# Attention and two feed-forward parts on one core: the second part's weights split early and kept in DRAM, the rests on VectorE, elu as a maximum

## The chip, the cores and the metric

One Trainium2 chip, of which the kernel uses one core with its five engines: TensorE (PE, with its weight loads as PEld), VectorE (DVE), ScalarE (ACT), GpSimd (POOL) and SyncE (SP), whose queue issues all of this kernel's DMAs. The metric is the device time of one execution in microseconds (us); several runs give a median.

## The reference

Attention with rotary positions runs over 4 batches of 8 heads with 576 tokens of 64 values. Its result, 2304 tokens of 512 values, goes through two feed-forward parts. The weights are float64, everything else is float32.

```python
x = attention(q, k, v)                              # 2304 x 512
h = x @ w_in                                        # 512 -> 2048
g = np.where(h > 0.0, h, np.exp(np.minimum(h, 0.0)) - 1.0)   # elu
x = (g @ w_out).astype(np.float32)                  # 2048 -> 512
a, b = x @ w1, x @ w2                               # 512 -> 1024 each
out = ((a * b @ w3) @ w_out2).astype(np.float32)    # 1024 -> 1024 -> 512
```

## The kernel before

Every float32 operand of TensorE stands as two tiles, the upper 12 bits (hi) and the exact rest (lo), and three matmuls (hi·hi, hi·lo, lo·hi) make one product. The matrix `w3 @ w_out2` (called W) is made once, so that the second part is `((x @ w1) * (x @ w2)) @ W`.

Weights come as 64-bit words, in parts of 128 partitions by 512 words (512 KB). `weight_steps` turns a part into its hi and lo in six steps: `rebase` on ScalarE (L104), `shift`, `low` and `sign` on VectorE (L107, L110, L113), `high` on ScalarE (L117) and `rest`, a subtraction, on GpSimd (L121). Three working tiles `wr` are shared by all parts; the result goes into the buffer that held the raw words.

The program has three stages.

- Attention: 16 units (pairs of heads) of 9 slots each, in an order written out by hand. GpSimd turns q and k here. Along with it the first parts of `w_in` and `w_out` are fetched and split, one every 9 slots from slot 10 on (`paced`); the constant `PF` says for how many of the 16 columns f of the first part both weights are made here, 5 before.
- First feed-forward part: five tiles of tokens (512, 512, 512, 384, 384), each with 16 slots f. `part_h` makes 128 columns of h (12 matmuls, L532) and the elu: a minimum on VectorE (L543), exp and minus one on ScalarE (L544, L545), a maximum and sum on VectorE (L547), then the split of g, hi on ScalarE (L77) and lo (L73) on GpSimd in the first tile of tokens and on VectorE in the others. `part_y` adds the product with `w_out` (12 matmuls, L559) for the slot before. In the first tile of tokens the remaining parts of `w_in` and `w_out` are loaded and split (`load_in_out`).
- In the last tile of tokens all 40 parts of the second feed-forward part's weights are loaded into the buffers that `w_in` and `w_out` leave, and split there: 8 of `w_out2` (`load_o`), 16 of `w3` (`load_3`), 8 each of `w1` and `w2` (`load_ab`). `part_w` makes a block of rows of W (24 matmuls, L590) in each of the last 8 slots. The second feed-forward part follows, with 24 matmuls for a and b (L532) and 12 or 9 for y (L647) a slot.

In the two feed-forward stages the order on each engine is not the program's: a scheduler places the instructions when the kernel is built, by its own table of costs. On the chip each engine then takes its instructions in just that order, so an instruction that waits holds up all that stands behind it on its engine; the same holds for DMAs on SP's queue.

Of the kernel before, what the change touches and what calls it, by code (L numbers as in the profile page):

```python
# [7 lines left out]
F32 = mybir.dt.float32  # L8
# [10 lines left out]
P = 128  # L19
NKC = 5  # parts of the keys, 128 and at the end 64  # L20
SK = S + 64  # the keys with the last 64 of them in front once more
SCALE = 1.0 / 8.0
SIGN = -(2**31)
PAIRS = ((0, 0), (0, 1), (1, 0))  # the products of (hi, lo) with (hi, lo) that float32 keeps

# Slots of a unit (a pair of heads) in the attention, counted from its first: 4 parts of the queries for each head, and
# the last 64 queries of both. Work on the unit itself:
NORM = (2, 7)  # reciprocals of the sums, of the first 256 queries and of the others
SPREAD = (3, 9)  # their broadcast over d
NTURN = (5, 11)  # its transpose  # L30
PV = (
    (5, 0, (0,)), (6, 0, (1,)), (7, 0, (2, 3)), (8, 0, (4,)),
    (10, 1, (0,)), (11, 1, (1,)), (12, 1, (2, 3)), (13, 1, (4,)),
)  # slot, part of the queries, parts of the keys
LOAD_V = 6  # and on those that follow it: loads, and the steps of the rope of k and q
LOAD_QK = 4
ROPE = ((-1, 0, 1, 1, 4), (-5, -4, -3, -3, 2))
STACK = 4
# The first unit, of which nothing runs ahead
FIRST = ((0, 1, 4), (0, 0, 0, 1, 2), (0, 0, 3, 3, 4), 2)  # L40
KD = 420  # keys from here on are turned by the second engine
WARM = 27
FILL = (4, 2, 2)
EVAC_ACT = (1, 0, 0, 1, 0, 0, 0, 0, 1, 0, 1, 0)  # which copies from PSUM are ScalarE's, in turn

# Weights: how many parts of w_in and w_out are split during the attention, from which slot on, and the steps' slots
PF, PF_AT, PF_STEP, STEPS, DLEAD = 5, 10, 9, (0, 1, 2, 2, 3, 8), 6
NA = 2 * PF
# In the last tile of tokens of the first feed-forward part: when the weights of the second are loaded, per part of f
LOAD_O = (0, 1, 1, 2, 3, 3, 4, 5)  # L50
LOAD_3, PART_W, LOAD_AB, AB_STEP = 5, 8, 10, 2
DEEP = 3  # parts of w3 held at once


@with_exitstack
def kernel(
# [9 lines left out]
    w_pools = [wa_p]  # L66
    wr_p = ctx.enter_context(tc.tile_pool(name="wr", bufs=3))

    def split(dst, src, hi_eng, lo_eng):
        """dst[:, 0] = src to 12 bits, dst[:, 1] = the exact rest."""  # L70
        hi, lo = dst[:, 0], dst[:, 1]
        copy_hi(hi, src, hi_eng)
        lo_eng.tensor_tensor(lo, src, hi.bitcast(F32), op=ALU.subtract)  # L73
# [16 lines left out]

    def weight_steps(at_, raw, put):
        """Float64 words to two tiles' worth of float32: 12 bits of 24, and the rest.

        The high word read as float32 has a float64 exponent's upper 8 bits: times 2**-112 it is
        rebased by -896 (what is too small for float32 goes to 0), and 3 bits to the left it is
        float32's layout, without the sign."""
        words = raw.bitcast(I32).rearrange("p (n t) -> p n t", t=2)
        lo, hi = words[:, :, 0], words[:, :, 1]
        r = wr_p.tile([P, 512], F32, tag="wr", name="wr")
        i = r.bitcast(I32)  # L100
        made = []

        def rebase():
            act.activation(r, hi.bitcast(F32), ACTF.Abs, scale=2.0**-112)  # L104

        def shift():
            dve.tensor_scalar(i, i, 3, None, op0=ALU.logical_shift_left)  # L107

        def low():
            dve.scalar_tensor_tensor(i, lo, 29, i, op0=ALU.logical_shift_right, op1=ALU.bitwise_or)  # L110

        def sign():
            dve.scalar_tensor_tensor(i, hi, SIGN, i, op0=ALU.bitwise_and, op1=ALU.bitwise_or)  # L113

        def high():
            made.append(slot(at_, F32R, [P, 2, 512], "w"))
            act.activation(made[0][:, 0], r, ACTF.Copy)  # L117
            put(made[0])

        def rest():  # L120
            pool.tensor_tensor(made[0][:, 1], r, made[0][:, 0].bitcast(F32), op=ALU.subtract)  # L121

        return rebase, shift, low, sign, high, rest

    def load_w(i, src, to, key):
        for f in weight_steps(i, fetch_w(i, src), lambda t: to.__setitem__(key, t)):
            f()
# [6 lines left out]

    # ------------------------------------------------ attention, and w3 @ w_out
    with ExitStack() as c1:
# [35 lines left out]
        def rope(u, w):  # L172
            """Steps of the turn of q or k by their positions, and of its split."""
            if u not in hls:
# [20 lines left out]
        def first_load(u):  # L195
            """In the order of their use: the first half of the scores, the other, and the other queries."""
            for w in (0, 1):
# [7 lines left out]
        def part(u, w, at_, to, eng, hi_eng, lo_eng):  # L205
            """Steps for some columns; the scale goes with the split."""
            s, c, t = (SCALE, 1.0)[w], COLS[w].start, TAB[w].start
# [34 lines left out]
        def diagonal(u):  # L242
            """The last 64 queries of each head, against its own keys only."""
            for j in range(2):
                h = slice(64 * j, 64 * j + 64)
                copy_hi(diag[units.index(u) % 2][h, :, h], hls[u][h, :, 512:S].bitcast(F32), pool)

        def stack(u):
            """Of each head [128 = (q_hi, q_lo)], [k_hi, k_lo] and [k_lo, k_hi], on the partitions."""
            st = stacks[u] = st_p.tile([P, 2, 3, S], F32R, tag="st", name="st")  # L250
# [9 lines left out]

        # ---- attention: of a pair of heads 128 queries each, and then the 64 last of both at once
        HALF = ((0, 256), (256, 320))
        sums_t, S_t, pr_t, pt_t = {}, {}, {}, {}

        def scores(g):
            u, c, j = g
            s = S_t[g] = ps_s.tile([P, 2, 512], F32, tag="s", name="s")
            if c == 4 or u == units[0]:
                # the halves one by one: of both heads with the diagonal, or of one
                d, h = diag[units.index(u) % 2], slice(64 * j, 64 * j + 64) if c < 4 else slice(0, P)  # L270
# [133 lines left out]
        def paced(n, i_, to, key, src):  # L404
            """The weights of src, fetched ahead of slot n, and the split's steps in the slots from there."""
            steps, raw = [], []
# [4 lines left out]
            def step(i):  # L411
                if i == 0:
                    steps.extend(weight_steps(i_, raw[0], lambda t: to.__setitem__(key, t)))
                steps[i]()
# [52 lines left out]
        def warm_up(n):  # L467
            """Keeps TensorE's clock up while it would wait."""
            ps = ps_t.tile([P, 512], F32, tag="pt", name="warm") if n else None
            for _ in range(n):  # L470
                pe.matmul(ps[:, :P], warm, warm, start=True, stop=True)
# [34 lines left out]

    # ------------------------------------------------ the two feed-forward parts
    with ExitStack() as c2:
        pool2 = lambda name, bufs: c2.enter_context(tc.tile_pool(name=name, bufs=bufs, reuse_waits="tile"))
        xt_p = pool2("xt", 4)  # L510
        w_pools.append(pool2("w", 1))
        g_p = pool2("g", 2)
        e_p = pool2("e", 2)
# [13 lines left out]
        def project(ps, w, x, n):  # L527
            """ps = (w as [c, 128 of f]).T @ x"""
            i = 0
# [8 lines left out]
        def part_h(ti, f, x):  # L538
# [3 lines left out]
            e = e_p.tile([P, n], F32, tag="e", name="e", padded_shape=[P, 512])  # L542
            dve.tensor_scalar(e, ps[:, :n], 0.0, None, op0=ALU.min)  # L543
            act.activation(e, e, ACTF.Exp)  # L544
            act.activation(e, e, ACTF.Copy, bias=-1.0)  # L545
            g = e
            dve.scalar_tensor_tensor(g, ps[:, :n], 0.0, e, op0=ALU.max, op1=ALU.add)  # L547
            t = g_p.tile([P, 2, n], F32R, tag="g", name="g", padded_shape=[P, 2, 512])
            split(t, g, act, dve if ti else pool)
            gs[ti, f] = t  # L550
# [19 lines left out]
        wo, w3_t = {}, {}  # L570

        def load_ab(f):
            i = 16 + 2 * DEEP + 2 * f
            i = i if i < 32 else i - 24
            load_w(i, w1[f], wa, f)
            load_w(i + 1, w2[f], wb, f)

        def load_o(j):
            load_w(j, w_o2[j], wo, j)

        def load_3(i):
            for z in range(2):
                load_w(8 + 2 * (i % DEEP) + z, w3[i][:, 512 * z:512 * z + 512], w3_t, (i, z))

        def part_w(i):
            """Rows of w3 @ w_o2."""
            ps = ps_h.tile([P, 512], F32, tag="h", name="w")
# [20 lines left out]
        for n, (ti, f) in enumerate(seq):  # L608
# [5 lines left out]
            if n >= 1:  # L614
                part_y(*seq[n - 1])
            for task, i in tasks.pop(n - len(seq) + NF, ()):
                task(i)
# [112 lines left out]
```

## Time and profile before

| | |
|---|---|
| time, median of 3 runs (lowest, highest) | 1089.44 us (1088.63, 1090.51) |
| span of the profiled execution | 1087.1 us |
| time beside the span (median less span) | 2.3 us |
| PE / PEld busy | 96% / 80% |
| DVE / ACT / POOL busy | 57% / 43% / 34% |
| HBM read / written | 64.68 MB / 4.72 MB |

The profile gives the profiled execution's span, from its first to its last instruction; no other time of that execution is on the page, so the time that lies around it is taken as the difference to the median. The page's busy share of PE counts a matmul from its start to its modelled end, including time in which it overlaps the next, so the pitch at which matmuls follow one another says more than the share. Attention ends at about 317 us, the first feed-forward part at about 788 us.

### The profile page before, as it was taken

To read this page: it belongs to the slowest core of one execution; us is meant where nothing else is said; L and a number is where in the kernel's file an instruction comes from. 1 tells how busy PE (TensorE), PEld (TensorE's weight loads), DVE (VectorE), ACT (ScalarE), POOL (GpSimd) and SP (SyncE) were. 2 spreads that over 40 slices of the span, in tenths; PEclk is the share of its full clock that TensorE was granted. 3 is DMA by queue.
4 is the path that set the end of the run, shared out by engine and by line. 5 is a ranking of instruction groups with operands and counts; after the bars stand their busy time and mean duration, and the time that the engine had idled before them with its cause. 6 is when DMAs were issued, how large, how long until landed. Compare 5 with 4: busy or idle time off the path is not lost. (4 is left out here: it accounts for less than half of the span.)

```text
span 1087.1 us, 14661 instructions
## 1 busy us (share of the span) xinstructions
PE 1048.0 (96%) x5590; PEld 865.3 (80%) x5590; DVE 621.9 (57%) x982; ACT 467.3 (43%) x921; POOL 365.4 (34%) x336
## 2 busy tenths in 40 slices
PE   9999999999998789999999999889899999999998
PEld 7777677677766568888888999778788888889997
DVE  5778788777659975335335346997971313122211
ACT  3566667666636554334334335654451111112121
POOL 5788898877226551001000001343450000000000
PEclk7899999999999999999999999999999999999999
DMA  5777787867481000000000005446500100001000
GB/s 164 207 223 222 216 226 224 220 195 198 120 339 48 0 1 1 1 1 1 1 1 1 1 1 159 122 127 190 159 20 1 39 1 25 15 1 39 1 30 30
DMA packets 34870, 96.90 MB, mean 89 GB/s; under 512 B 4208, under 2 KB 5872, under 8 KB 34800
## 3 DMA queue, kind: packets, MB, share of 16 engines
q1 hardware_dynamic: 34800, 95.96, 29.6%
q8 instruction: 44, 0.72, 0.3%
q14 instruction: 26, 0.21, 0.1%
HBM read 64.68 MB, written 4.72 MB: 64 GB/s over the span
## 5 line engine op out<-in xcount | busy, mean ns | idle before, releaser
L559 PE MATMUL y<-g,w 128*128 128x512 f32 (+1 forms) x960 | 218.0, 374 | 23.8 <-ACT g L77 16.8
L559 PEld LDWEIGHTS y<-g,w 128*128 128x128 f32 x960 | 176.3, 191 | 54.8 <-ACT g L77 22.0
L532 PE MATMUL h<-xt,w 128*128 128x512 f32 (+1 forms) x960 | 212.2, 368 | 1.1 <-DVE e L547 1.1
L532 PEld LDWEIGHTS h<-xt,w 128*128 128x128 f32 x960 | 175.1, 188 | 24.8 <-DVE e L547 1.5
L73 POOL TENSOR_TENSOR xt<-xT,xt 128x512 fp32r<-128x512 f32 (+1 forms) x20 | 25.5, 1273 | 446.1 <-DVE xt L79 446.1
L298 ACT ACTIVATE pr<-s,nm 128x576 f32<-128x576 f32 x144 | 107.0, 743 | 101.8 <-DVE nm L294 100.9
L121 POOL TENSOR_TENSOR w<-wr,w 128x512 fp32r<-128x512 f32 x72 | 102.5, 1424 | 124.6 <-ACT w L117 119.8
L294 DVE TENSOR_REDUCE nm<-s 128x1 f32<-128x576 f32 x144 | 108.6, 754 | 24.8 <-PE s L282 12.0
L634 DVE TENSOR_TENSOR a<-b,a 128x512 f32<-128x512 f32 (+1 forms) x40 | 25.5, 637 | 157.5 <-PE b L532 156.8
L532 PE MATMUL a<-xt,w 128*128 128x512 f32 (+1 forms) x480 | 107.8, 368 | 2.7 <-DVE xt L73 2.7
L532 PE MATMUL b<-xt,w 128*128 128x512 f32 (+1 forms) x480 | 106.8, 367 | 0.0
L647 PE MATMUL y<-W,g 128*128 128x512 f32 x432 | 105.2, 391 | 0.2 <-DVE g L73 0.2
L544 ACT ACTIVATE e<-e 128x512 f32<-128x512 f32 (+1 forms) x80 | 47.0, 588 | 135.7 <-DVE e L543 135.6
L532 PEld LDWEIGHTS a<-xt,w 128*128 128x128 f32 x480 | 88.1, 188 | 15.5 <-DVE xt L73 3.1
L330 PEld LDWEIGHTS ptp<-idt,pr 128*128 128x128 f32 x576 | 63.4, 144 | 46.2 <-issue 24.7
L282 PE MATMUL s<-st 128*128 128x288 f32 x480 | 95.1, 316 | 4.0 <-DMA st<-hl 3.8
L532 PEld LDWEIGHTS b<-xt,w 128*128 128x128 f32 x480 | 87.6, 188 | 11.3
L330 PE MATMUL ptp<-idt,pr 128*128 128x128 f32 x576 | 96.4, 291 | 0.0
L647 PEld LDWEIGHTS y<-W,g 128*128 128x128 f32 x432 | 80.8, 188 | 16.7 <-DVE g L73 0.6
L543 DVE TENSOR_SCALAR e<-h 128x512 f32<-128x512 f32 (+1 forms) x80 | 50.6, 633 | 63.1 <-PE h L532 62.9
L547 DVE SCALAR_TENSOR_TENSOR e<-h,e 128x512 f32<-128x512 f32 (+1 forms) x80 | 50.7, 634 | 57.7 <-ACT e L545 57.7
L180 POOL TENSOR_TENSOR raw_qk<-raw_qk,tab 128x640 f32<-128x640 f32 (+1 forms) x56 | 82.5, 1482 | 2.3
(302 smaller groups left out, 1371.1 us busy)
## 6 DMA issues: line engine op xcount, KB each, us to landing
st<-hl SPq DMA_DIRECT2D x60, 288.0 KB, 4.5
raw<-w_ SPq DMA_DIRECT2D x32, 512.0 KB, 4.1
raw_qk<-k_ SPq DMA_DIRECT2D x15, 640.0 KB, 5.7
raw_qk<-q_ SPq DMA_DIRECT2D x15, 576.0 KB, 5.2
st<-hl SPq DMA_DIRECT2D x60, 144.0 KB, 4.2
raw<-w_in_ SPq DMA_DIRECT2D x16, 512.0 KB, 5.1
raw<-w_out_ SPq DMA_DIRECT2D x16, 512.0 KB, 5.8
out_<-ev SPq DMA_DIRECT2D x18, 256.0 KB, 2.1
```

Source lines behind the costliest of these rows:

```text
L121: pool.tensor_tensor(made[0][:, 1], r, made[0][:, 0].bitcast(F32), op=ALU.subtract)
L180: pool.tensor_tensor(r[:, z], r[:, z], tab[:, w, z, TAB[w]], op=ALU.mult)
L282: pe.matmul(s[:, n, :288], st[:, j, 0, c * P:c * P + P], st[:, j, z, n * 288:(n + 1) * 288], start=(z == 1), stop=(z == 2),)
L294: dve.tensor_reduce(nm, s[:, :, :288], axis=AX.XY, op=ALU.max, negate=True)
L298: act.activation(pr_t[u, c][:, j].rearrange("p (n i) -> p n i", n=2), s[:, :, :288], ACTF.Exp, bias=nm, accum_out=sums_t[u, hf][:, at_:at_ ...
L330: pe.transpose(pt[:, kc], pr[:, at_:at_ + P], idt)
L532: pe.matmul(ps[:, :n], w[:, a, cc * P:(cc + 1) * P], x[cc][:, c], start=(i == 0), stop=(i == 11))
L543: dve.tensor_scalar(e, ps[:, :n], 0.0, None, op0=ALU.min)
L544: act.activation(e, e, ACTF.Exp)
L547: dve.scalar_tensor_tensor(g, ps[:, :n], 0.0, e, op0=ALU.max, op1=ALU.add)
L559: pe.matmul(ys[ti][o][:, :n], wout[f][:, a, o * P:(o + 1) * P], g[:, c], start=(f == 0 and i == 0), stop=(f == NF - 1 and i == 2),)
L647: pe.matmul(outs[ti][o], g[:, a, o * P:(o + 1) * P], wW[f][:, c], start=(f == 0 and i == 0), stop=(f == NG - 1 and i == 2),)
```

## The change

- The sign, shift and other steps of a weight part stay; the `rest` of weights that are split in the feed-forward stages goes to VectorE (in attention it stays on GpSimd). The lo half of g is VectorE's in the first tile of tokens too.
- The elu becomes `max(exp(min(h, 0)) - 1, h)`: a ReLU of -h and an exp on ScalarE, and one pass on VectorE.
- `PF` goes from 5 to 6: 12 parts of `w_in` and `w_out` are split in attention, 20 are left for the first tile of tokens.
- The 40 parts of the second feed-forward part's weights are fetched and split one a slot from slot 17 of the 80 on (`early`), through a ring of three buffers (`stage`) that raw words and results share, and the result is written to DRAM. In the last tile of tokens `load_o`, `load_3` and `load_ab` only load it back (`again`).

```diff
-PF, PF_AT, PF_STEP, STEPS, DLEAD = 5, 10, 9, (0, 1, 2, 2, 3, 8), 6
+PF, PF_AT, PF_STEP, STEPS, DLEAD = 6, 10, 9, (0, 1, 2, 2, 3, 8), 6
+EARLY, EARLY_STEP, STAGES = 17, 1, 3
...
         def high():
-            made.append(slot(at_, F32R, [P, 2, 512], "w"))
+            made.append(stage_p.tile([P, 2, 512], F32R, tag="stage", name="w") if at_ is None else
+                        slot(at_, F32R, [P, 2, 512], "w"))
...
         def rest():
-            pool.tensor_tensor(made[0][:, 1], r, made[0][:, 0].bitcast(F32), op=ALU.subtract)
+            rest_eng.tensor_tensor(made[0][:, 1], r, made[0][:, 0].bitcast(F32), op=ALU.subtract)
...
-            dve.tensor_scalar(e, ps[:, :n], 0.0, None, op0=ALU.min)
-            act.activation(e, e, ACTF.Exp)
-            act.activation(e, e, ACTF.Copy, bias=-1.0)
+            act.activation(e, ps[:, :n], ACTF.Relu, scale=-1.0)
+            act.activation(e, e, ACTF.Exp, scale=-1.0)
             g = e
-            dve.scalar_tensor_tensor(g, ps[:, :n], 0.0, e, op0=ALU.max, op1=ALU.add)
+            dve.scalar_tensor_tensor(g, e, -1.0, ps[:, :n], op0=ALU.add, op1=ALU.max)
...
-            split(t, g, act, dve if ti else pool)
+            split(t, g, act, dve)
...
+        def early(key, src):
+            raw = stage_p.tile([P, 512], I64, tag="stage", name="raw")
+            nc.sync.dma_start(raw, src)
+            done = {}
+            for f in weight_steps(None, raw, lambda t: done.__setitem__(0, t), dve):
+                f()
+            kept[key] = kept_p.tile([P, 2, 512], F32, tag="kept_%s_%d_%d" % key, name="kept")
+            nc.sync.dma_start(kept[key], done[0].bitcast(F32))
+        def again(i, key, to, at_):
+            to[at_] = slot(i, F32R, [P, 2, 512], "w")
+            nc.sync.dma_start(to[at_].bitcast(F32), kept[key])
...
         def load_o(j):
-            load_w(j, w_o2[j], wo, j)
+            again(j, ("o", j, 0), wo, j)
...
             if n >= 1:
                 part_y(*seq[n - 1])
+            if n >= EARLY and (n - EARLY) % EARLY_STEP == 0 and ahead:
+                early(*ahead.pop(0))
```

The new kernel's lines have other numbers: in it L110 is the shift of a weight part, L113 low, L116 sign and L125 the rest; L552 is the elu's pass on VectorE, L76 the lo half of g, L582 the fetch and L587 the store of an early part.

On VectorE in the first tile of tokens, a piece of the kernel before (shift, low and sign of weight parts, and the elu's two passes L543 and L547):

```order
L107 TENSOR_SCALAR wr<-wr 128x512
L110 SCALAR_TENSOR_TENSOR wr<-raw,wr 128x512
L113 SCALAR_TENSOR_TENSOR wr<-raw,wr 128x512
L107 TENSOR_SCALAR wr<-wr 128x512
L543 TENSOR_SCALAR e<-h 128x512
L547 SCALAR_TENSOR_TENSOR e<-h,e 128x512
L110 SCALAR_TENSOR_TENSOR wr<-raw,wr 128x512
```

The same place now (`w` is a weight part, `g` the elu's result):

```order
L110 TENSOR_SCALAR wr<-wr 128x512
L125 TENSOR_TENSOR w<-wr,w 128x512
L116 SCALAR_TENSOR_TENSOR wr<-raw,wr 128x512
L76 TENSOR_TENSOR g<-e,g 128x512
L113 SCALAR_TENSOR_TENSOR wr<-raw,wr 128x512
L110 TENSOR_SCALAR wr<-wr 128x512
L552 SCALAR_TENSOR_TENSOR e<-e,h 128x512
L125 TENSOR_TENSOR w<-wr,w 128x512
```

The rests (L125) and the lo half of g (L76) stand between the other passes, and each elu has one pass (L552) where it had two.

On VectorE from the second tile of tokens on, where before nothing of weights stood, the pattern is now (one early part a slot; every few slots a second elu stands between two parts):

```order
L110 TENSOR_SCALAR wr<-wr 128x512
L113 SCALAR_TENSOR_TENSOR wr<-raw,wr 128x512
L116 SCALAR_TENSOR_TENSOR wr<-raw,wr 128x512
L552 SCALAR_TENSOR_TENSOR e<-e,h 128x512
L125 TENSOR_TENSOR w<-wr,w 128x512
L76 TENSOR_TENSOR g<-e,g 128x512
```

The elu and the lo half of g of a slot stand behind passes that wait for an early part's words; the first early rest is placed behind the 14th elu of 80 and the 40th behind the 60th, 40 parts beside 46 elus.

On SP's queue the early parts stand as a fetch and a store in turn:

```order
L582 DMA raw<-w_o_ 128x512 x2
L587 DMA kept<-w 128x1024
L582 DMA raw<-w_o_ 128x512
L587 DMA kept<-w 128x1024
L582 DMA raw<-w_o_ 128x512
```

Two fetches go ahead; from then on a fetch waits for the store of the part two before it, whose buffer it takes, and the next store stands behind it.

## Rows read from the trace of the kernel before

**Rows 1.** The page's head and its busy times.

```profile
span 1087.1 us, 14661 instructions
PE 1048.0 (96%) x5590; PEld 865.3 (80%) x5590; DVE 621.9 (57%) x982; ACT 467.3 (43%) x921; POOL 365.4 (34%) x336
```

**Rows 2.** Busy time of each engine by stretches (first the stretch and its length, then busy us and number of instructions, and at the end the granted clock, the DMA share and GB/s): the end of attention to the end of weight work in the first tile of tokens; from there to the last tile; the last tile and the start of the second part; the rest.

```profile
317.37:403.15 85.78, 69.47 (x291) 52.79 (x288) 79.25 (x95) 50.42 (x85) 51.16 (x35) 1.00 0.14 53
403.15:671.20 268.05, 268.05 (x1293) 235.73 (x1292) 119.88 (x187) 103.60 (x180) 15.82 (x12) 1.00 0.03 10
671.20:816.40 145.20, 133.57 (x631) 116.01 (x630) 126.47 (x176) 74.87 (x135) 59.05 (x41) 0.98 0.43 129
816.40:1087.10 270.70, 266.18 (x1260) 231.01 (x1259) 66.74 (x105) 46.37 (x82) 9.24 (x8) 1.00 0.05 18
```

**Rows 3.** Pieces of the chain of work that ended last (start us, us, what): twelve matmuls over 512 columns and twelve over 384.

```profile
816.39 2.72 PE a L532 x12
...
999.07 2.10 PE a L532 x12
```

**Rows 4.** The first stretch again, of PE's matmuls alone: those of line 532 (h), then those of line 559 (y).

```profile
317.37:403.15 85.78, 36.39 (x143) 1.00 0.14 53
...
317.37:403.15 85.78, 37.91 (x144) 1.00 0.14 53
```

**Rows 5.** Groups of PE's matmuls in the third stretch, by shape (number, busy us, mean ns, idle time before them).

```profile
L590 PE MATMUL w<-w 128*128 128x512 f32 x192 | 45.8, 391 | 0.2 <-ACT w L117 0.2
L559 PE MATMUL y<-g,w 128*128 128x384 f32 x169 | 37.1, 363 | 8.5 <-DVE g L73 6.3 <-ACT g L77 2.2
L532 PE MATMUL h<-xt,w 128*128 128x384 f32 x137 | 26.2, 336 | 0.0
L532 PE MATMUL a<-xt,w 128*128 128x512 f32 x49 | 12.6, 392 | 2.7 <-DVE xt L73 2.7
L532 PE MATMUL b<-xt,w 128*128 128x512 f32 x48 | 11.5, 389 | 0.0
L647 PE MATMUL y<-W,g 128*128 128x512 f32 x36 | 9.0, 393 | 0.2 <-DVE g L73 0.2
```

**Rows 6.** Groups of VectorE in the first stretch, by shape; the last row is from the second stretch, the lo half of g where GpSimd is silent.

```profile
L110 DVE SCALAR_TENSOR_TENSOR wr<-raw,wr 128x512 int32<-128x512 int32 x22 | 23.6, 1075 | 0.2
L107 DVE TENSOR_SCALAR wr<-wr 128x512 int32<-128x512 int32 x22 | 21.5, 982 | 0.0
L113 DVE SCALAR_TENSOR_TENSOR wr<-raw,wr 128x512 int32<-128x512 int32 x22 | 20.8, 947 | 0.2
L547 DVE SCALAR_TENSOR_TENSOR e<-h,e 128x512 f32<-128x512 f32 x14 | 9.5, 683 | 4.0 <-ACT e L545 4.0
L543 DVE TENSOR_SCALAR e<-h 128x512 f32<-128x512 f32 x14 | 9.4, 681 | 1.9 <-PE h L532 1.9
...
L73 DVE TENSOR_TENSOR g<-e,g 128x512 fp32r<-128x512 f32 x32 | 22.1, 692 | 20.9 <-ACT g L77 20.2
```

**Rows 7.** The timeline of ScalarE, VectorE and GpSimd (start us, us, what): one weight part that meets no other, its rebase, shift, low, sign, high and rest.

```profile
661.59 0.67 ACT L104 ACTIVATE wr<-raw 128x512 f32<-128x512 f32 x1
662.49 0.42 DVE L107 TENSOR_SCALAR wr<-wr 128x512 int32<-128x512 int32 x1
662.94 0.69 DVE L110 SCALAR_TENSOR_TENSOR wr<-raw,wr 128x512 int32<-128x512 int32 x1
663.66 0.69 DVE L113 SCALAR_TENSOR_TENSOR wr<-raw,wr 128x512 int32<-128x512 int32 x1
664.39 0.64 ACT L117 ACTIVATE w<-wr 128x512 fp32r<-128x512 f32 x1 [0.70 <-DVE wr L113]
665.11 1.30 POOL L121 TENSOR_TENSOR w<-wr,w 128x512 fp32r<-128x512 f32 x1 [11.19 <-ACT w L117]
```

**Rows 8.** The timeline of GpSimd and of VectorE in the first tile of tokens: two passes of GpSimd and the VectorE passes that run beside them.

```profile
336.75 1.49 POOL L121 TENSOR_TENSOR w<-wr,w 128x512 fp32r<-128x512 f32 x1
341.92 1.33 POOL L73 TENSOR_TENSOR g<-e,g 128x512 fp32r<-128x512 f32 x1 [0.38 <-ACT g L77]
...
337.11 1.68 DVE L110 SCALAR_TENSOR_TENSOR wr<-raw,wr 128x512 int32<-128x512 int32 x1
342.01 1.52 DVE L107 TENSOR_SCALAR wr<-wr 128x512 int32<-128x512 int32 x1
```

**Rows 9.** Who waited for whom over the whole span (us in total, times, longest): PE's waits in the two feed-forward stages.

```profile
PE y L559 <- ACT g L77: 16.8, 10, 3.1
PE a L532 <- DVE xt L73: 2.7, 1, 2.7
```

**Rows 10.** From issue to landing: the 512 KB weight loads of the last tile of tokens, then the 256 KB writes of the result.

```profile
DMA to landing us min/median/max: 3.4/4.1/5.5
...
DMA to landing us min/median/max: 2.0/2.1/3.3
```

**Rows 11.** Busy times by stretches of 25 us in attention, as in rows 2: two with weight parts beside it and two without.

```profile
175.00:200.00 25.00, 24.39 (x174) 17.30 (x173) 19.10 (x35) 16.24 (x38) 22.05 (x21) 1.00 0.87 230
200.00:225.00 25.00, 24.33 (x177) 18.12 (x176) 19.20 (x37) 17.65 (x43) 21.00 (x23) 1.00 0.64 186
225.00:250.00 25.00, 24.62 (x181) 17.76 (x179) 17.44 (x32) 14.98 (x36) 20.52 (x21) 1.00 0.80 217
250.00:275.00 25.00, 25.00 (x186) 18.73 (x183) 17.89 (x35) 17.06 (x39) 19.38 (x21) 1.00 0.62 168
```

More of the change, by code (lines that the diff above doesn't have):

```diff
@@ L67 @@
     wr_p = ctx.enter_context(tc.tile_pool(name="wr", bufs=3))
+    kept_p = ctx.enter_context(tc.tile_pool(name="kept", bufs=1, space=bass.MemoryType.DRAM))
     def split(dst, src, hi_eng, lo_eng):
@@ L89, in fetch_w, with weight_steps @@
         return raw
-    def weight_steps(at_, raw, put):
+    def weight_steps(at_, raw, put, rest_eng):
         words = raw.bitcast(I32).rearrange("p (n t) -> p n t", t=2)
@@ L120, in rest @@
         def rest():
-            pool.tensor_tensor(made[0][:, 1], r, made[0][:, 0].bitcast(F32), op=ALU.subtract)
+            rest_eng.tensor_tensor(made[0][:, 1], r, made[0][:, 0].bitcast(F32), op=ALU.subtract)
         return rebase, shift, low, sign, high, rest
     def load_w(i, src, to, key):
-        for f in weight_steps(i, fetch_w(i, src), lambda t: to.__setitem__(key, t)):
+        for f in weight_steps(i, fetch_w(i, src), lambda t: to.__setitem__(key, t), dve):
             f()
@@ L412, in step @@
                 if i == 0:
-                    steps.extend(weight_steps(i_, raw[0], lambda t: to.__setitem__(key, t)))
+                    steps.extend(weight_steps(i_, raw[0], lambda t: to.__setitem__(key, t), pool))
                 steps[i]()
@@ L511 @@
         w_pools.append(pool2("w", 1))
+        stage_p = pool2("stage", STAGES)
         g_p = pool2("g", 2)
@@ L570 @@
         wo, w3_t = {}, {}
+        kept = {}
+        def early(key, src):
[9 more added lines that the diff above has]
+            nc.sync.dma_start(to[at_].bitcast(F32), kept[key])
         def load_ab(f):
@@ L574, in load_ab @@
             i = i if i < 32 else i - 24
-            load_w(i, w1[f], wa, f)
-            load_w(i + 1, w2[f], wb, f)
+            again(i, ("a", f, 0), wa, f)
+            again(i + 1, ("b", f, 0), wb, f)
         def load_o(j):
-            load_w(j, w_o2[j], wo, j)
+            again(j, ("o", j, 0), wo, j)
         def load_3(i):
             for z in range(2):
-                load_w(8 + 2 * (i % DEEP) + z, w3[i][:, 512 * z:512 * z + 512], w3_t, (i, z))
+                again(8 + 2 * (i % DEEP) + z, ("3", i, z), w3_t, (i, z))
+        ahead = [(("o", j, 0), w_o2[j]) for j in range(8)]
+        ahead += [(("3", i, z), w3[i][:, 512 * z:512 * z + 512]) for i in range(8) for z in range(2)]
+        ahead += [t for f in range(NG) for t in ((("a", f, 0), w1[f]), (("b", f, 0), w2[f]))]
         def part_w(i):
@@ L720 @@
     }
-    nc = bacc.Bacc("TRN2", target_bir_lowering=False, num_devices=1)
+    nc = bacc.Bacc("TRN2", target_bir_lowering=False, num_devices=1, dynamic_dma_scratch_size=2048)
     args = [
```

## The prediction

> **What bounds the kernel now.** I read the page's busy times first, then stretches of the span, then the groups and the timeline in the stretches where something is lost. PE is busy 96% of 1087.1 us [rows 1], so the first question is how much of that is pitch and how much is waiting. The chain that ended last shows the pitch where nothing disturbs it: twelve matmuls over 512 columns take 2.72 us, 0.2267 us each, and twelve over 384 columns 2.10 us or a little less, on average 0.1735 us each over a slot [rows 3]. A slot of the first part (24 matmuls) is therefore 5.44 us at 512 tokens and 4.16 us at 384.
>
> Held against the stretches [rows 2], two lose time. From 317.37 to 403.15 us PE did 143 + 144 matmuls over 512 columns [rows 4]; at 0.2267 us these need 65.1 us, and they took 85.78, so 20.7 us are lost. From 671.20 to 816.40 it did 306 matmuls over 384 columns and 325 over 512 [rows 5]: 306 x 0.1735 + 325 x 0.2267 = 126.8 us in 145.2, so 18.4 us are lost. In the second and the fourth stretch PE has no gap worth the name: it is busy 268.05 of 268.05 and 266.18 of 270.70 us, the latter with its tail. So 39.1 us can be had, in two places, and nothing elsewhere after attention.
>
> Both are the stretches in which weight parts are split, and in both VectorE is the full engine: 79.25 of 85.78 us and 126.47 of 145.20 [rows 2]. The reader is to see two things in its groups. Shift, low and sign take 982, 1075 and 947 ns on average in the first stretch [rows 6], but 0.42, 0.69 and 0.69 us for a part that meets nobody [rows 7]. And the long ones stand beside a pass of GpSimd: a low of 1.68 us beside GpSimd's pass of 1.49 us, a shift of 1.52 us beside one of 1.33 us [rows 8]. The elu's passes, which read PSUM, keep their 681 and 683 ns in the same stretch [rows 6]. So what is lost is not that VectorE has too much to do but that GpSimd's passes hold its weight passes up, and the elu behind them in the same queue is late. PE waits for g: 16.8 us in ten waits, the longest 3.1 [rows 9].
>
> **The first tile of tokens.** GpSimd's rests and its lo half of g go to VectorE. Each costs 0.69 us there (0.692, the lo half of g in quiet, rows 6). VectorE's bill for the tile was 22 parts and the elus, 84.8 us by the five groups of rows 6. Now it is 20 parts x (0.42 + 3 x 0.69) = 49.8 us and 16 slots x 2 x 0.69 = 22.1 us, together 71.9 us for 16 slots of PE, 87.0 us. VectorE is no longer full. The elu's chain loses one VectorE pass (0.68) and keeps three ScalarE passes. As a cover for what stays late at the start and in the queue I keep one wait of the longest kind, 3.1 us [rows 9]. The stretch gives 20.7 - 3.1 = 17.6 us; from 20.7 (nothing late) down to -10 (the second rival).
>
> **The last tile of tokens.** 40 x 2.49 us of VectorE and 40 passes of GpSimd leave it; only loads of the same 512 KB stay. They take 4.1 us [rows 10] and have time: the last buffer that W's first block needs is free four slots of 4.16 us before it is used, and the w3 buffers come round after three blocks of W. The switch to the second part needs x split on VectorE; that wait was 2.7 us [rows 9], and I keep it. 18.4 - 2.7 = 15.7 us; bounds 18.4, and 10 if the first two blocks of W each wait for a load of 4.1 us.
>
> **Attention.** Two more parts take 18 slots; 144 slots take 317 us, so 18 are 40 us. PE did 174 and 177 instructions in 25 us with weights beside it, 181 and 186 without [rows 11]: 4.4% of 40 us, +1.7 us, from 0 to 3.
>
> **The early parts.** This is the new cost. By work alone there is room: a part adds 2.49 us to VectorE, which with 2 x 0.69 of elu makes 3.87 of 5.44 us, and 1.3 to ScalarE; DMA was at 3% [rows 2]. What can bind is the ring of three buffers. A fetch waits for the store of the part two before, so two parts pass in the time of one round: fetch, six steps, store. The fetch is 4.1 us (3.4 to 5.5, rows 10). The steps from the start of rebase to the end of high are 3.44 us, and 0.08 + 0.69 for the rest, 4.2 us [rows 7]; elu passes that stand between them add none to two of 0.60, I take 0.9. The store has no row. A 256 KB write lands in 2.1 us; 512 KB cannot be faster than the 2.0 that was the fastest, and at twice the length it is 4.2 [rows 10]; I take the middle, 3.1. Four handovers of about 0.1 make 0.4. Sum 12.7 us a round, between 9.9 and 15.5.
>
> The order on VectorE ties 40 parts to 46 elus, so a round has 2 x 46/40 = 2.3 slots, 12.5 us (at 384 columns eight parts beside twelve elus, three slots, 12.5 again). A shorter round costs nothing, since the ring then waits for PE. A longer one holds the elu behind a pass that waits for words, and PE with it: each us above 12.5 costs 20 us over 20 rounds. At 12.7 it is 4 us; the bounds are 0 and 60.
>
> The Trainium skill (DMA: Bandwidth & Descriptors, section Measured under Bandwidth) gives 6.15 us for 1 MB from HBM and 0.95 for 64 KB, issued another way; an estimate between them for 512 KB is 3.4 us. As the price of the store it would make the round 13.0 us and the loss 10 us; the trace has no such store.
>
> **The sum.** Against the profiled span: 1087.1 - 17.6 - 15.7 + 1.7 + 4 = 1059.5 us. Around it lie 2.3 us, the median of 1089.44 less the span. Forecast 1062 us (1061.8).
>
> **The rivals.**
>
> The ring binds in part: a round of 13.0 to 14.2 us. For it speaks that my sum already lies at the limit and that fetch and store share SP's queue, each store standing behind a fetch that waits. Against it, the fetch need not meet another one: with one store and one fetch in 6.2 us it should land nearer to 3.4. Loss 10 to 34 us instead of 4, so 1068 to 1092, more likely in the lower half.
>
> Slower than before: the ring binds in full, at a fetch of 5.5 us, a store of 4.2, two elu passes in between: 15.5 us. Then 20 x 3.0 = 60 us are lost and the span is 1115.5, the time 1118. The point from which it decides is where the loss eats 17.6 + 15.7 - 1.7 = 31.6 us, a round of 14.1 us. The rows of the loads speak against it: 5.5 is the longest of all, taken while two or more loads ran together. The Trainium skill (DMA: Bandwidth & Descriptors, Latency and other measured facts) puts HBM's access latency at 0.2 us on average and 2 us under high load; by that rule, with fetch and store both 1.8 us longer, a round would be 16.3 us and this rival true. No run here shows a loaded store; DMA at 3% before and some 170 GB/s now is less than the 230 GB/s that attention moves [rows 11].
>
> VectorE stays slow: its weight passes are long for another reason than GpSimd (the 64-bit stride of the raw words). Then the first tile costs 20 x (0.98 + 1.08 + 0.95 + 0.69) + 22.1 = 96 us, 10 more than now, and the time is 1087.1 + 10.3 - 15.7 + 1.7 + 4 + 2.3 = 1090, no change. Against it stands the part of rows 7, with the same stride and short passes.
>
> **How the numbers follow.** Forecast 0.70; ring in part 0.20; ring in full 0.06; VectorE slow 0.04. The best case, nothing lost anywhere and no price in attention, is 1087.1 - 39.1 + 2.3 = 1050.3; I begin the range at 1051. Upwards it takes in most of the ring in part, to 1079. Two runs of one kernel differ by up to 0.2% here, so that is what a measurement can tell from no change: 1087.3 to 1091.6. Faster: the forecast, nearly all of the ring in part and some of the slow VectorE, 0.92; same 0.03; slower 0.05.
>
> **What would show it.** In the profile after: shift, low and sign at 0.42, 0.69 and 0.69 us after attention, and no GpSimd there but for x; PE at 110 matmuls per 25 us from 325 us on; in the last tile no weight passes on VectorE and blocks of W without gaps; stores that land in about 3 us. The forecast is wrong if ScalarE's rebase waits for fetches (a wait of rebase for `raw` of more than a few us in total) and PE's count falls between the second and the fourth tile of tokens, which is the ring, or if PE still waits for g in the first tile.

## The result: 1089.04 to 1052.45 us, and the profile after

The new kernel takes 1052.45 us, the median of four runs (1051.51 to 1053.71); the kernel before took 1089.04 us on the same chip (1086.97 to 1090.51). The ratio is 0.9666, 95% interval [0.9646, 0.9686]. The forecast was 1062 us with a range from 1051 to 1079.

The head of the new kernel's page and its busy times, beside [rows 1], and its bytes:

```profile
span 1050.8 us, 14641 instructions
...
PE 1037.8 (99%) x5590; PEld 865.4 (82%) x5590; DVE 568.3 (54%) x978; ACT 463.7 (44%) x921; POOL 257.9 (25%) x260
...
HBM read 85.66 MB, written 25.69 MB: 106 GB/s over the span
```

PE's 5590 matmuls are the same and fill 99% of a span that is 36.3 us shorter. GpSimd is busy 107.5 us less. The 40 stores and the 40 loads back add 21 MB in each direction. The profiled run took 1052.59 us, so 1.8 us lie around the span.

Busy times by stretches (the columns of [rows 2]): the first tile of tokens, the second to the middle of the fourth, the rest of the fourth, the last tile with the start of the second part, and the rest.

```profile
320.00:400.00 80.00, 80.00 (x354) 66.04 (x353) 74.03 (x131) 54.05 (x95) 3.27 (x2) 1.00 0.21 77
400.00:580.00 180.00, 180.00 (x805) 150.26 (x804) 123.50 (x202) 102.80 (x176) 5.88 (x4) 1.00 0.52 181
580.00:672.00 92.00, 92.00 (x533) 92.00 (x532) 44.25 (x78) 42.28 (x83) 2.29 (x2) 1.00 0.43 149
672.00:817.00 145.00, 145.00 (x685) 125.62 (x684) 34.45 (x52) 28.93 (x52) 5.47 (x4) 1.00 0.30 98
817.00:1050.80 233.80, 229.29 (x1098) 200.52 (x1096) 56.80 (x90) 41.44 (x74) 6.82 (x6) 1.00 0.06 21
```

In the first line PE issues 354 matmuls in 80 us; at the undisturbed pitch of [rows 3], 0.2267 us, 80 us hold 353. So nothing is lost, although VectorE still works 74 of 80 us. In the last tile, the fourth line, VectorE falls to 34 of 145 us.

VectorE's groups in the first tile of tokens, 317 to 395 us (the view of [rows 6]):

```profile
L113 DVE SCALAR_TENSOR_TENSOR wr<-raw,wr 128x512 int32<-128x512 int32 x22 | 16.2, 735 | 0.0
L116 DVE SCALAR_TENSOR_TENSOR wr<-raw,wr 128x512 int32<-128x512 int32 x22 | 15.1, 686 | 0.0
L125 DVE TENSOR_TENSOR w<-wr,w 128x512 fp32r<-128x512 f32 x22 | 15.1, 686 | 0.7 <-ACT w L121 0.7
L552 DVE SCALAR_TENSOR_TENSOR e<-e,h 128x512 f32<-128x512 f32 x15 | 10.2, 683 | 2.8 <-ACT e L550 2.6
L110 DVE TENSOR_SCALAR wr<-wr 128x512 int32<-128x512 int32 x22 | 9.3, 422 | 0.4 <-ACT wr L107 0.4
```

Shift 422 ns for 982, low 735 for 1075, sign 686 for 947: the durations of the lone part of [rows 7], now with 22 parts in a row. Low's mean is above 0.69 us because one of its passes, beside GpSimd's split of x at 391 us, took 1.78 us. The elu's pass has not changed (683).

The weights' transfers on the page (KB each, and at the end the median us from issue to landing): stores, loads back, and fetches of early parts (32 of the 40).

```profile
kept<-w SPq DMA_DIRECT2D x40, 512.0 KB, 2.6
w<-kept SPq DMA_DIRECT2D x40, 512.0 KB, 3.3
...
raw<-w_ SPq DMA_DIRECT2D x32, 512.0 KB, 3.6
```

Waits over the whole span (total, times, longest): all of PE's own, then those of ScalarE's rebase (L107) for a fetch.

```profile
PE s L286 <- DMA st<-hl: 4.3, 10, 0.9
PE s L278 <- ACT hl L80: 3.0, 1, 3.0
PE warm L475 <- DVE warm L486: 1.1, 1, 1.1
...
ACT wr L107 <- DMA raw<-w_: 18.8, 17, 2.9
...
ACT wr L107 <- DMA raw<-w_o_: 3.7, 3, 1.6
```

PE's three waits all lie in attention; the waits for g and for x of [rows 9] are gone. Rebase does wait for words, 22.5 us in 20 waits, but PE has no wait from it. A piece of SP's queue shows how close that is:

```profile
440.80 0.33 SPq L587 DMA_DIRECT2D kept<-w  x1
443.42 0.33 SPq L582 DMA_DIRECT2D raw<-w_  x1
447.18 0.33 SPq L587 DMA_DIRECT2D kept<-w  x1
449.82 0.33 SPq L582 DMA_DIRECT2D raw<-w_  x1
```

Each fetch goes out 2.62 and 2.64 us behind a store, which is when that store has landed (2.6 us). Of 36 fetches of the ring 26 do so within 0.2 us. So the fetches wait for the ring of buffers, and still every part is ready before PE needs what stands behind it.

### The profile page after: what moved, and what is told of

It reads as the page before. It is cut to its first block, busy times and chain, and to the rows that moved or that the text cites. A ratio compares the mean times of both kernels' runs of the same rounds, so it can differ in the third digit from the quotient of the medians.

```text
span 1050.8 us, 14641 instructions
## 1 busy us (share of the span) xinstructions
PE 1037.8 (99%) x5590; PEld 865.4 (82%) x5590; DVE 568.3 (54%) x978; ACT 463.7 (44%) x921; POOL 257.9 (25%) x260
## 4 chain that ended last, share of the span: by engine, by line
PE 90%; SPq 3%; DMA 3%; DVE 1%; POOL 1%; issue 1%; ACTq 0%; ACT 0%; DVEq 0%
PE h L537 19%; PE y L564 19%; PE a L537 9%; PE b L537 9%; PE y L674 9%; PE ptp L334 6%; PE o L392 5%; PE s L286 5%; PE w L615 4%; DMA st<-hl 3%; PE s L278 2%; SPq L263 2%; SPq L260 1%; PE o L394 1%; POOL hl L193 1%
## 5 line engine op out<-in xcount | busy, mean ns | idle before, releaser
L564 PE MATMUL y<-g,w 128*128 128x512 f32 (+1 forms) x960 | 212.5, 367 | 0.0
L564 PEld LDWEIGHTS y<-g,w 128*128 128x128 f32 x960 | 175.2, 188 | 22.5
L76 POOL TENSOR_TENSOR xt<-xT,xt 128x512 fp32r<-128x512 f32 (+1 forms) x20 | 26.5, 1326 | 668.9 <-DVE xt L82 668.1
L537 PEld LDWEIGHTS a<-xt,w 128*128 128x128 f32 x480 | 88.2, 188 | 12.5
L659 ACT ACTIVATE a<-a 128x512 f32<-128x512 f32 (+1 forms) x40 | 22.3, 556 | 139.2 <-PE a L537 139.2
L552 DVE SCALAR_TENSOR_TENSOR e<-e,h 128x512 f32<-128x512 f32 (+1 forms) x80 | 50.3, 631 | 61.1 <-ACT e L550 60.7
L549 ACT ACTIVATE e<-h 128x512 f32<-128x512 f32 (+1 forms) x80 | 44.2, 554 | 72.6 <-PE h L537 70.2
L286 PEld LDWEIGHTS s<-st 128*128 128x128 f32 x480 | 67.9, 189 | 7.0 <-issue 3.8
```

What stands on the lines that cost most here:

```text
L286: pe.matmul(s[:, n, :288], st[:, j, 0, c * P:c * P + P], st[:, j, z, n * 288:(n + 1) * 288], start=(z == 1), stop=(z == 2),)
L537: pe.matmul(ps[:, :n], w[:, a, cc * P:(cc + 1) * P], x[cc][:, c], start=(i == 0), stop=(i == 11))
L549: act.activation(e, ps[:, :n], ACTF.Relu, scale=-1.0)
L552: dve.scalar_tensor_tensor(g, e, -1.0, ps[:, :n], op0=ALU.add, op1=ALU.max)
L564: pe.matmul(ys[ti][o][:, :n], wout[f][:, a, o * P:(o + 1) * P], g[:, c], start=(f == 0 and i == 0), stop=(f == NF - 1 and i == 2),)
```

## Where the time is counted

The start of the program is not the same in every execution. PE's granted clock falls between 10 and 40 us, by different amounts. For before and after, the 27th row maximum of attention on VectorE and the last matmul of attention (start us, us, what) show what this does; first the kernel before:

```profile
71.57 0.76 DVE L294 TENSOR_REDUCE nm<-s 128x1 f32<-128x576 f32 x1
...
317.11 0.33 PE L393 MATMUL o<-plT,v__3599 64*64 64x64 f32 x4
```

and the new kernel:

```profile
73.68 0.76 DVE L298 TENSOR_REDUCE nm<-s 128x1 f32<-128x576 f32 x1
...
319.31 0.33 PE L397 MATMUL o<-plT,v__3621 64*64 64x64 f32 x4
```

Attention ends 2.2 us later in the new kernel, but 2.1 of these are there already at the 27th row maximum. So beside the medians I use a second number for each kernel: the span of its profiled execution less the end of its last attention matmul. For before this is 1087.1 - 317.44 = 769.7 us, for after 1050.8 - 319.64 = 731.2 us: the feed-forward stages are 38.5 us shorter.

Each ratio is to runs of the kernel before on the same chip as that kernel's; their medians lie between 1087.9 and 1089.2 us.

| kernel | median us | ratio to before, 95% interval | after attention, us |
|---|---|---|---|
| before | 1089.04 | | 769.7 |
| after | 1052.45 | 0.9666 [0.9646, 0.9686] | 731.2 |
| e1 after, rests on GpSimd | 1064.17 | 0.9795 [0.9753, 0.9837] | 745.2 |
| e2 after, no early split | 1051.87 | 0.9662 [0.9627, 0.9697] | 731.3 |
| e3 before, rests on VectorE | 1061.68 | 0.9751 [0.9731, 0.9771] | 740.2 |
| e4 after, old elu | 1052.98 | 0.9673 [0.9639, 0.9706] | 733.2 |
| e5 after, PF 5 | 1051.03 | 0.9651 [0.9629, 0.9673] | 731.6 |
| e6 after, two ring buffers | 1078.01 | 0.9903 [0.9887, 0.9920] | 759.6 |
| e7 after, no early split, PF 5 | 1050.85 | 0.9659 [0.9643, 0.9676] | 731.1 |
| e8 only the early split | 1079.26 | 0.9914 [0.9895, 0.9933] | 758.2 |
| e9 after, GpSimd passes added that nobody needs | 1080.75 | 0.9925 [0.9897, 0.9954] | 759.6 |
| e10 e7 with PF 4 | 1052.68 | 0.9674 [0.9648, 0.9699] | 732.7 |
| e11 after, PF 4 | 1052.41 | 0.9666 [0.9638, 0.9695] | 731.8 |

## The experiments

**e1: the weights' rests back on GpSimd in the feed-forward stages.** The first tile's lo half of g stays on VectorE.

```diff
-        for f in weight_steps(i, fetch_w(i, src), lambda t: to.__setitem__(key, t), dve):
+        for f in weight_steps(i, fetch_w(i, src), lambda t: to.__setitem__(key, t), pool):
...
-            for f in weight_steps(None, raw, lambda t: done.__setitem__(0, t), dve):
+            for f in weight_steps(None, raw, lambda t: done.__setitem__(0, t), pool):
```

> The changed kernel, but the rests of the weights in both feed-forward stages on GpSimd again. Theory (GpSimd's passes hold up VectorE's weight passes): shift, low and sign go from 0.42, 0.69, 0.69 us back to about 1.0 us each in the first tile of tokens, VectorE is full there and PE waits for g; 1060 to 1072 us. Rival (VectorE only had too much to do): it has 0.69 us less per part, so the time stays at 1052 or falls.

Measured 1064.17 us. VectorE's groups and the stretches of e1 in the first tile:

```profile
L116 DVE SCALAR_TENSOR_TENSOR wr<-raw,wr 128x512 int32<-128x512 int32 x23 | 25.2, 1097 | 0.2
...
L110 DVE TENSOR_SCALAR wr<-wr 128x512 int32<-128x512 int32 x23 | 14.1, 613 | 2.2 <-ACT wr L107 2.2
L76 DVE TENSOR_TENSOR g<-e,g 128x512 fp32r<-128x512 f32 x14 | 11.8, 840 | 2.4 <-ACT g L80 2.2
```

```profile
350.00:375.00 25.00, 20.33 (x84) 14.85 (x82) 24.76 (x32) 15.15 (x26) 12.00 (x9) 1.00 0.00 0
375.00:400.00 25.00, 21.90 (x90) 16.56 (x91) 19.23 (x26) 14.20 (x25) 8.94 (x7) 1.00 0.26 90
```

GpSimd works 12 of 25 us again, VectorE's passes are long and PE does 84 and 90 matmuls where 110 fit. 14.0 us of the 38.5 are lost again after attention. They are lost in the first tile, where VectorE is full; from 403 to 650 us, where the rests of the early parts are GpSimd's too and VectorE works 150 of 247 us, PE loses nothing. This alone does not say whether VectorE is held up or the rests merely come late; e9 does.

**e9: GpSimd busy with work that nobody needs.** The program is the new one; GpSimd has 48 subtractions more, right behind attention, on a tile of its own.

```diff
+        beside = pool2("beside", 1).tile([P, 512], F32, name="beside")
+        pool.memset(beside, 0.0)
...
+            if n < 16:
+                for _ in range(3):
+                    pool.tensor_tensor(beside, beside, beside, op=ALU.subtract)
             part_h(ti, f, x[ti])
```

> The new kernel with 48 subtractions on GpSimd added right behind attention, back to back, on a tile of its own that nobody reads: the result and every dependency are as they were, only GpSimd is busy for some 48 x 1.3 to 1.5 = 62 to 72 us of the first tile of tokens. Theory (GpSimd's passes lengthen VectorE's passes that run beside them and read SBUF only): shift well above 0.42, low, sign, the rest and the lo half of g at 0.85 to 1.1 us in that time, the elu's pass L552, which reads PSUM, still at 0.69; VectorE is then full, as 20 x (0.98 + 1.08 + 0.95 + 1.0) + 16 x (0.69 + 1.0) = 107 us of work do not fit into 87 us, PE falls below 112 matmuls in 25 us and the time is 1060 to 1075 us. Rival (the run with the rests on GpSimd again was slower because those rests come late, 1.3 us instead of 0.69 and in another queue, and not because VectorE is held up): passes as in the new kernel and 1051 to 1054 us.

Measured 1080.75 us, beyond the 1075 that the theory gave: the passes took up to 1.28 us on average, not 0.85 to 1.1. One stretch of e9, VectorE's groups from 320 to 400 us (lines were added, so the elu's pass is L554 here), and GpSimd's group from 310 to 420 us with its shortest, median and longest pass:

```profile
350.00:375.00 25.00, 16.56 (x58) 11.76 (x58) 25.00 (x23) 9.86 (x17) 23.59 (x19) 0.86 0.00 1
...
L116 DVE SCALAR_TENSOR_TENSOR wr<-raw,wr 128x512 int32<-128x512 int32 x14 | 17.9, 1281 | 0.0
L113 DVE SCALAR_TENSOR_TENSOR wr<-raw,wr 128x512 int32<-128x512 int32 x16 | 16.8, 1055 | 0.0
L125 DVE TENSOR_TENSOR w<-wr,w 128x512 fp32r<-128x512 f32 x13 | 16.4, 1263 | 0.0
L110 DVE TENSOR_SCALAR wr<-wr 128x512 int32<-128x512 int32 x16 | 13.9, 877 | 0.0
L76 DVE TENSOR_TENSOR g<-e,g 128x512 fp32r<-128x512 f32 x10 | 12.7, 1269 | 0.0
L554 DVE SCALAR_TENSOR_TENSOR e<-e,h 128x512 f32<-128x512 f32 x11 | 7.3, 675 | 0.0
...
L642 POOL TENSOR_TENSOR beside<-beside 128x512 f32<-128x512 f32 x48 | 62.1, 1293 | 3.8
...
L642 POOL TENSOR_TENSOR beside<-beside x48: 1041/1367/1371, 320.4 to 384.8; 128x512 f32<-128x512 f32 x48
```

A piece of its timeline for VectorE, and GpSimd's in the same 6 us:

```profile
339.37 1.52 DVE L116 SCALAR_TENSOR_TENSOR wr<-raw,wr 128x512 int32<-128x512 int32 x1
340.82 1.52 DVE L113 SCALAR_TENSOR_TENSOR wr<-raw,wr 128x512 int32<-128x512 int32 x1
342.26 1.52 DVE L76 TENSOR_TENSOR g<-e,g 128x512 fp32r<-128x512 f32 x1
...
338.98 8.33 POOL L642 TENSOR_TENSOR beside<-beside 128x512 f32<-128x512 f32 x6
```

Nothing depends on these passes, and still VectorE's passes over two SBUF operands take 1.52 us instead of 0.69 and start every 1.45 us, about one per pass of GpSimd (8.33 / 6 = 1.39). The elu's pass, one operand of which is in PSUM, keeps its 675 ns. GpSimd pays too, but less: the first two of its passes, beside which VectorE's read mostly PSUM, took 1.04 us, and the median, with passes over two SBUF operands beside it, 1.37. In the kernel before, likewise, its rests took 1.27 to 1.75 us in the first tile, against the 1.30 of [rows 7]. So GpSimd's passes do hold VectorE's up, with no dependency between them, and PE falls to 58 matmuls where 110 fit (at a granted clock of 0.86). That settles the cause.

The Trainium skill (GPSIMD Engine Reference, section 1. Specifications) says that GpSimd shares its SBUF interfaces with VectorE, so that it contends with VectorE instructions that have two SBUF inputs or run in a two-port mode; low, sign, rest and lo half (two SBUF inputs) agree, and so does the elu's pass, which has one; that the shift, with one input, runs in such a mode is not shown by a run here, only that 422 ns become 877.

**e3: the kernel before with the rests and the first tile's lo half of g on VectorE, nothing else.**

```diff
-            pool.tensor_tensor(made[0][:, 1], r, made[0][:, 0].bitcast(F32), op=ALU.subtract)
+            rest_eng.tensor_tensor(made[0][:, 1], r, made[0][:, 0].bitcast(F32), op=ALU.subtract)
...
-            split(t, g, act, dve if ti else pool)
+            split(t, g, act, dve)
```

> The kernel before with one edit: in the feed-forward stages the rests of the weights, and the lo half of g in the first tile of tokens, on VectorE instead of GpSimd. Theory: VectorE's passes get short, its bill is 88 us for 87 in the first tile and about 138 for 127 in the last; some 3 and 12 of the 39 us stay lost: 1060 to 1070 us. Rival (too much work on VectorE): 0.69 us more per part on the full engine, slower than before, 1095 us or more.

Measured 1061.68 us: this edit alone brings 29.5 of the 38.5 us after attention. What is left shows in two stretches of e3, in the first and in the last tile:

```profile
375.00:400.00 25.00, 23.95 (x102) 18.65 (x101) 24.31 (x43) 13.97 (x23) 2.52 (x2) 1.00 0.00 0
...
675.00:700.00 25.00, 22.29 (x111) 19.94 (x111) 24.32 (x47) 15.27 (x27) 0.00 (x0) 1.00 0.39 119
```

GpSimd is silent and the passes are short, but VectorE, with two elu passes a slot, is full by its own work (24.3 of 25 us), and PE still falls behind a little. Over the whole span VectorE does 78 passes more than in the kernel before and is busy less, 605.0 us for 621.9.

**e2: the new kernel without the early split.** The last tile fetches and splits the 40 parts as before; PF is 6, the rests are VectorE's, the elu is the new one.

```diff
-EARLY, EARLY_STEP, STAGES = 17, 1, 3
+EARLY, EARLY_STEP, STAGES = 999, 1, 3
...
-            again(i, ("a", f, 0), wa, f)
-            again(i + 1, ("b", f, 0), wb, f)
+            load_w(i, w1[f], wa, f)
+            load_w(i + 1, w2[f], wb, f)
```

(`load_o` and `load_3` likewise.)

> The changed kernel without the early split: the 40 parts of the second part's weights are loaded and split in the last tile of tokens as before, with the rests on VectorE; nothing goes through DRAM. Theory: without GpSimd VectorE needs 40 x 2.49 + 16 x 1.11 us and some 10 us for W and x, 127 us for 127 us of matmuls, so it just about keeps up and a part of the 18.4 us stays lost: 1056 to 1064 us. Rival (the early split alone gives the gain of the last tile): all 18 us are lost again, 1070 us or more.

Measured 1051.87 us, against what I expected. The last tile of e2:

```profile
675.00:700.00 25.00, 24.98 (x124) 22.14 (x123) 23.21 (x44) 15.58 (x27) 0.00 (x0) 1.00 0.37 116
...
725.00:750.00 25.00, 25.00 (x124) 22.23 (x124) 24.17 (x45) 14.09 (x26) 2.64 (x2) 1.00 0.74 218
```

VectorE is 93 and 97% busy in these stretches and PE loses nothing. With short passes and one elu pass less, the splits fit into the last tile; moving them away gains nothing more.

**e4: the new kernel with the old elu,** its minimum on VectorE, two passes on ScalarE and the maximum and sum on VectorE.

> The changed kernel with the elu as before (minimum and maximum-plus on VectorE, exp and minus one on ScalarE). Theory: VectorE has 0.69 us more per slot, 83 us of 87 in the first tile and 4.56 of 5.44 us a slot beside an early part, 4.14 of 4.16 at 384 tokens; PE is hardly touched: 1053 to 1059 us. Rival (the shorter elu chain is what keeps PE fed): 1065 us or more.

Measured 1052.98 us; after attention 733.2, 2.0 more than after. So the new elu is worth some 2 us beside the early split, and 9.1 without it (e3 to e7, 740.2 to 731.1): the two edits take load from the same engine, and with the rests moved either gives nearly all of it. The rival of this run, that PE needs the shorter chain of the elu, is out.

**e5: the new kernel with PF 5.**

> The changed kernel with 10 weight parts in attention, as before, and 22 in the first tile of tokens. Theory: VectorE needs 22 x 2.49 + 22.1 = 77 us of 87 in the first tile, so PE still does not wait, and attention gets back what two parts cost it, 1 to 2 us: 1050 to 1052 us. Rival (the first tile needs the sixth column made ahead, since VectorE is full at its start): PE waits for g or for weights, 1056 us or more.

Measured 1051.03 us, 731.6 after attention.

**e7: of the change only the rests on VectorE and the new elu** (e2 with PF 5).

> The changed kernel without the early split and with 10 weight parts in attention: of the change only the rests on VectorE and the new elu are left. Theory: VectorE still has just enough time in both tiles, and attention is 1 to 2 us shorter: 1049 to 1052 us. Rival (the early split or the sixth column is needed): 1057 us or more.

Measured 1050.85 us, 731.1 after attention: two edits give the whole gain, without the DRAM buffers, the ring and 42 MB of traffic.

**e8: of the change only the early split,** with PF 5, the old elu, and the rests and the first tile's lo half on GpSimd.

> Of the change only the early split through DRAM: the rests and the lo half of g in the first tile stay on GpSimd, the elu is the old one, 10 parts in attention. Theory: the last tile of tokens loses nothing, 18 us back; the first tile loses its 20 us as before, a few more where GpSimd's rests meet VectorE beside the early parts: 1070 to 1078 us. Rival (the early split carries the change): 1062 us or less.

Measured 1079.26 us, a little above what was expected. The last tile loses nothing (PE 50.00 of 50 us in each 50 us from 650 to 800), but the first one loses as before: 78 and 77 matmuls from 350 to 375 and from 375 to 400 us. It loses longer, too: from 400 to 425 us, where the kernel before did 112 matmuls again, e8 did 92. So 11.5 us come back after attention and not 18.4.

**e6: the ring with two buffers.**

```diff
-EARLY, EARLY_STEP, STAGES = 17, 1, 3
+EARLY, EARLY_STEP, STAGES = 17, 1, 2
```

> The changed kernel with a ring of two buffers instead of three; VectorE's order ties 40 parts to 46 elus again. Theory (a round longer than its slots holds the elu and PE up): a fetch now starts when the sign of the part before is done; fetch 3.6, rebase to sign 2.8, elu passes between them 0.9, handovers 0.3, so 7.6 us a part where 1.15 slots are 6.3: 40 x 1.3 = 52 us lost, 1095 to 1110 us. Rival (the ring's waits fall into slack that the elu has anyway): under 1058 us.

Measured 1078.01 us, 28.4 more after attention, between the theory and the rival. A stretch beside early parts, and waits over the span:

```profile
400.00:580.00 180.00, 166.09 (x699) 130.16 (x699) 105.57 (x171) 86.23 (x149) 3.35 (x2) 0.99 0.45 152
```

```profile
ACT wr L107 <- DMA raw<-w_: 70.2, 32, 3.7
...
ACT wr L107 <- DMA raw<-w_o_: 15.2, 7, 3.0
PE y L564 <- ACT g L80: 14.8, 18, 2.3
```

This is what a ring that binds looks like: rebase waits 85.4 us, PE waits for g again (its weight loads too), and 699 matmuls stand where the new kernel has 805. The stores of all 40 parts are issued from 383.0 to 647.0 us, 264.0 / 39 = 6.77 us a part; with three buffers from 387.7 to 619.3, 5.94 a part. The 0.83 us between them make 32 us over 39 parts, near the 28.4 lost. I had summed 7.6 a part for two buffers, more than the ring takes. Here many a store goes out 1.4 us behind a fetch, and stores land in 3.6 us (median); with three buffers, mostly alone, in 2.6.

**e10 and e11: PF 4,** without and with the early split.

> Of the change only the rests on VectorE and the new elu, and four columns of the first part split in attention instead of five: two weight parts leave attention, each worth about 0.9 to 1.1 us there by the 2.2 us that attention grew with two more, and VectorE's bill for the first tile rises by 2 x 2.49 us, to 24 x 2.49 + 22 = 82 us of 87. If VectorE keeps up: 1048 to 1051 us, about 1 to 2 us less than with five. Rival: VectorE is full at the start of the first tile, PE waits for weights or for g and the time is 1053 us or more.

> The new kernel with four columns of the first part split in attention instead of six. The same bill on VectorE in the first tile of tokens (82 of 87 us), and the early parts begin in the second tile, so that a lag of VectorE would not be made up there as quickly. If VectorE keeps up: 1048 to 1051 us. Rival: PE waits for weights or g, 1053 us or more.

Measured 1052.68 and 1052.41 us. VectorE keeps up (24.34 and 24.81 of 25 us in e10 from 325 to 375 us, PE 112 matmuls in each), yet the 1 to 2 us did not come. From the start of the 27th row maximum to the end of attention e10 takes 244.3 us and e11 246.1, with the same attention code; with PF 5 five kernels (before, e3, e5, e7, e8) lie between 244.6 and 247.7, and with PF 6 another six (after, e1, e2, e4, e6, e9) between 244.7 and 248.0. What two weight parts cost in attention is smaller than this spread. Of all versions none is faster than the new kernel by more than the intervals; e7 is the simplest of the fastest.

## Why the prediction was right

**The cause and the 39.1 us.** The two stretches with their 20.7 and 18.4 us of loss were all that could be had: 38.5 us are gone after attention, and PE has no wait there. That GpSimd's passes hold VectorE's up was read from durations side by side [rows 6 to 8]; e9 shows it without any dependency.

**First tile, 17.6 us.** It gave all 20.7. The cover of 3.1 us that I kept for a late g was not needed: no wait of PE for g is left.

**Last tile, 15.7 us.** It gave all 18.4; the wait for x split, 2.7 us, is gone as well. The size was right, but the edit to which I gave it was not needed for it. I let the 18.4 us come from the 40 parts leaving the tile. e2 and e7 keep them there and lose nothing. I had worked out the cost of the passes under GpSimd for the first tile, and had not done the same sum for the last: 40 parts at 2.49 us are 99.6 us, 16 elus with one pass and the lo half 17.8 (the groups of 384 columns take 553 and 559 ns in the new kernel), 8 splits of W at 0.69 another 5.5, together 123 us for the 126.8 us of matmuls that the prediction counted there. It fits, but barely; the expectation of e2 came to 127 us by such a sum and still took a part of the loss to stay.

**Attention, +1.7 us.** It ended 2.2 us later, which looked like a hit and was not: 2.1 us of it are the start. The price of two more parts can't be told from none here.

**The ring, +4 us.** Nothing was lost, and that the term came out so near is luck: two errors offset each other. The terms of the round were the right ones and too large, a fetch 3.6 us for 4.1, a store 2.6 for 3.1. But the 12.5 us that a round was allowed were too long as well. That figure spreads the twelve elus beside the last eight parts, at 384 columns, over all forty. By the same counts the first 32 parts stand beside 34 elus, so that a round at 512 columns has 2.1 slots, 11.6 us. With that the 12.7 us summed would have lost 1.1 us in each of 16 rounds and 0.2 in four, some 18 us in place of 4, and the forecast would have been about 1076 us. The stores went out every 5.94 us, 11.9 us a round; since PE did not wait, that is the pace of PE's slots and not what a round needs. The seven quickest rounds, from a fetch to the next but one, took 10.2 to 10.9 us. The forecast named as the sign of a binding ring that rebase waits more than a few us and PE's count falls; the first happened (22.5 us), the second did not. The estimate from the Trainium skill's page (DMA: Bandwidth & Descriptors, Measured under Bandwidth), 3.4 us for the store, was longer than the 2.6 measured, and the loss of 10 us that followed from it is not there.

**The sum.** The three reserves, 3.1 + 2.7 + 4 = 9.8 us, are the difference between 1062 and 1052.45 almost by themselves, and the measured time lies only 1.5 us above the lower end of the range. The small rest is the start and the time around the span, 1.8 instead of 2.3 us.

**The rivals.** The ring in part, and in full: neither; e6 shows how near they were, one buffer less costs 28.4 us. The rule on HBM's latency under high load (the Trainium skill, DMA: Bandwidth & Descriptors, Latency and other measured facts) would have made fetch and store 1.8 us longer each; at the 181 GB/s of this stretch both are shorter than in the sum. Whether that is a high load in the page's sense no run here shows. VectorE slow for another reason: refuted, the passes are short with the same stride.

## What to carry to other kernels

Read the duration of one and the same pass in a quiet and in a crowded place; when it doubles beside GpSimd, moving GpSimd's work onto the "full" engine can make that engine emptier. When several edits relieve the same engine, their gains don't add: sum the engine's bill for each edit alone before paying for the costly one, here the trip through DRAM. And compare from a mark behind the part that varies from run to run.

## What was not expected of the hardware

That GpSimd's passes make VectorE's take about as long as their own, one for one (0.69 to 1.52 us), and are lengthened by less themselves (1.04 to 1.37 us, e9). And the clock: in the new kernel PE waited 3.0 us for the first k split at 9.6 us, and the granted clock, full until 10 us, fell to the lower of its two levels (1.2 of 2.4 GHz) for much of the time to 40 us. Stretches of PE in the new kernel, the clock third from the end:

```profile
10.00:20.00 10.00, 7.38 (x31) 6.46 (x32) 5.25 (x8) 2.36 (x6) 7.58 (x8) 0.60 0.27 91
20.00:30.00 10.00, 10.00 (x40) 8.33 (x38) 6.03 (x11) 3.92 (x10) 3.73 (x5) 0.50 0.39 123
```

and in e7, where the wait was 1.6 us:

```profile
10.00:20.00 10.00, 8.92 (x51) 7.44 (x51) 6.17 (x9) 3.72 (x10) 7.83 (x8) 0.83 0.33 113
20.00:30.00 10.00, 8.73 (x43) 5.76 (x41) 8.23 (x13) 5.54 (x13) 7.05 (x10) 0.77 0.66 180
```

e7's 27th row maximum starts at 67.90 us, the new kernel's at 73.68: 5.8 us, more than any of the smaller edits is worth. The wait alone does not tell how far the clock falls: the kernel before waited 1.6 us too, and its row maximum starts at 71.57. What decides it was not tried. In e9, too, the clock fell, to 0.80 to 0.86 from 325 to 400 us, where PE waited for VectorE; so part of its 28.4 us is the clock and not the passes alone.
